# One mask product for two query thirds at the start of a block-sparse attention and spatial-gating kernel

## The chip, the cores and the metric

The kernel runs on one core of a Trainium2 chip. The metric is the device time of one execution in microseconds (us), lower is better. Three runs of the kernel before gave 209.83, 210.31 and 210.68 us; their median is 210.31 us.

The engines go by these names: PE is TensorE's matrix product and PEld its weight load, DVE is VectorE, ACT is ScalarE, POOL is GpSimd, and SP issues most of the DMA loads and stores.

## The reference

There are two stages. The first is attention over 4 batches, 8 heads, 768 positions and 64 elements a head, with a mask of blocks of 32 positions: a query block sees its own block and the two next to it, the first and the last block, and three sampled ones; the first and the last query block see all keys.

```python
scores = scale * np.matmul(q, k.transpose(0, 1, 3, 2))
mask = np.abs(blk_i - blk_j) <= window
mask = mask | (blk_i == 0) | (blk_j == 0) | (blk_i == n_blocks - 1) | (blk_j == n_blocks - 1)
for qb in range(n_blocks):
    for kb in sampled_blocks[qb]:
        mask[qb * block:(qb + 1) * block, kb * block:(kb + 1) * block] = True
scores = np.where(mask, scores, -1000000000.0)
# softmax over keys, then attn @ v
```

The second is a gated feed-forward layer on the heads put side by side (512 wide): `h = relu(x @ w_in)`, halves `u` and `v` of 512 each, `v` normalized, mixed over positions by `w_spatial` plus a bias, `(u * v_s) @ w_out`.

## The kernel before

**The mask as extra rows of the scores.** The tile `kq` holds, for each of the 8 heads of a batch, the transposed keys in columns 0 to 767 (`K_`) and the transposed queries in columns 768 to 1535 (`Q_`); partitions 0 to 63 are the head's 64 elements. Partitions 64 to 87 (`MR`; up to 127 as `MX`, zeros above 87) are 24 mask rows. Under a key they hold a one in the row of the key's block. Under a query they hold what its block adds to each key block: 0 or -300. A product of 128 rows then gives scores with the mask in them. The mask rows are the same for all heads, so they are made once, in head 0, and copied to the others by `rows` (line 236).

**How the query mask rows come about.** `bm` (24 rows, 128 columns) is the table of key blocks against query blocks, made on VectorE from the sampled blocks (line 206). `mask_rows` (line 268) multiplies it on TensorE with the one-hot key rows of a third of the positions (`TW` = 256 columns; there are three thirds) and copies the product into head 0's query columns of that third. Lines 285 to 300 write this out by hand for the first two thirds. The first product takes its one-hot rows from head 1, whose upper 64 partitions GpSimd has set to zero in columns 0 to 255 (line 173); the second takes only the 24 mask rows, from head 0. The third third follows later, in slot 3, by VectorE.

**The start.** TensorE runs 26 fillers (`filler`, line 177: products of a zero tile with itself, which nobody reads), then, in program order: transposes of head 0's keys, two fillers, the first mask product, two fillers, transposes of head 0's queries, two fillers, the second mask product, and the first scores (line 400). VectorE copies the transposes into `kq` (`split0`, line 280). ScalarE casts the first keys, copies the one-hot rows into head 0, copies the first mask product, copies head 2's key rows (columns 0 to 511; line 290), copies the second mask product, and starts on the exponentials. GpSimd casts what the loads bring in, copies the query mask rows of both thirds to head 1 (line 299) and head 2's key rows, columns 512 to 767 (line 300).

**Loads.** SP issues them in the order of the list `ORDER` (line 302), four ahead of GpSimd's casts, which go through the same list: `k1` is the keys of pair 1 (heads 2 and 3), `q1a` the first third of its queries, `v0` the values of pair 0, then `k2`, `q2a` and so on.

**Slots.** From line 840 the program goes through slots. The first 36 (`S0`) are the first batch, with 1,024 scores a partition in each: products into a `sc` bank (two of them), one exponential on ScalarE (lines 403 and 413; 424 for later batches). Lines 717 to 757 put work behind slots: `second` and `third` (the other transposes of head 0 and head 1) at slots 0 and 1, fillers at 2, the transposes `tr_first` of pairs 1, 2 and 3 at slots 4, 6 and 10, and the copies of mask rows in the list `ROWS` (line 726), all on VectorE. One entry there, `(1, 3, 4, K_)`, copies the key rows to head 3 in slot 1. Products with the values (line 451) follow four slots behind the scores, and the second stage's products (lines 554 and 623) are dealt out between them. All engines take their instructions in the order in which the program lists them.

**PSUM.** Small products and transposes share two banks, moeA and moeB; `moe_tag()` (line 253) hands them out in turn.

Of the kernel before, what the change touches and what calls it, by code (L numbers as in the profile page):

```python
# [10 lines left out]
FP32 = mybir.dt.float32  # L11
# [15 lines left out]
def kernel(  # L27
# [16 lines left out]
    nc = tc.nc  # L44

    B, H, S, D = q.shape
# [14 lines left out]
    KR = D + NB  # L61
    NT = 3
    TC = NCH // NT
    TW = TC * 128
    S0 = NT * NG * 3
    MOE0 = 12
    FILL, FILL2, FILL3 = 26, (2, 2, 2), 3
    U_DVE = (0, 1, 2, 3, 4, 5)

    const = ctx.enter_context(tc.tile_pool(name="const", bufs=1))  # L70
# [1 line left out]
    psum = ctx.enter_context(tc.tile_pool(name="psum", bufs=1, space=bass.MemoryType.PSUM))  # L72
# [10 lines left out]
    kq = const.tile([128, H, 2 * S], BF16, name="kq")  # L83
    NVV = 6
    vv = [const.tile([128, 2, NCH, VA], BF16, name=f"vv{s}") for s in range(NVV)]
    MR = slice(D, KR)
    MX = slice(D, 128)
    K_, Q_ = slice(0, S), slice(S, 2 * S)

    def qcols(t0, n=1):  # L90
        return slice(S + t0 * TW, S + (t0 + n) * TW)
# [62 lines left out]
    bm = const.tile([KR, 128], BF16)  # L154
# [15 lines left out]
    for s in range(NVV):  # L170
        nc.gpsimd.memset(vv[s][:, :, :, D:VA], 1.0)
    nc.gpsimd.memset(mhalf, -0.5)
    nc.gpsimd.memset(kq[0:D, 1, 0:TW], 0.0)

    wps = psum.tile([128, 512], FP32, tag="av", bufs=2)

    def filler(n, to):
        for _ in range(n):
            nc.tensor.matmul(out=to[:, 0:128], lhsT=warm, rhs=warm, start=True, stop=True)
# [28 lines left out]
    PL, DV = nc.gpsimd, nc.vector  # L208
# [27 lines left out]
    def rows(hs, cs, eng=nc.vector):  # L236
        src = kq[MX, 0:1, cs].to_broadcast([MX.stop - MX.start, hs.stop - hs.start, cs.stop - cs.start])
        if eng is nc.scalar:
            nc.scalar.activation(out=kq[MX, hs, cs], in_=src, func=AF.Copy)
        else:  # L240
            eng.tensor_copy(out=kq[MX, hs, cs], in_=src)
# [11 lines left out]
    def moe_tag():  # L253
        moe_tags.rotate(1)
        if moe_tags[0] in held:
            moe_tags.rotate(1)
        return moe_tags[0]

    def bank(nm="ps", tag=None):
        return psum.tile([128, 1024], BF16, tag=tag or moe_tag(), bufs=2 if tag else 1, name=nm)  # L260
# [4 lines left out]
    def pair_of(src, c):  # L265
        return src[:, c].rearrange("p h d -> p (h d)")

    def mask_rows(ps, t, copy, h=0, rs=slice(0, KR)):
        nc.tensor.matmul(out=ps[:, 0:TW], lhsT=bm[rs], rhs=kq[rs, h, t * TW:(t + 1) * TW],
                         start=True, stop=True)  # L270
        copy(kq[MX, 0, qcols(t)], ps[0:MX.stop - MX.start, 0:TW])


    def head(ps, h, c0, n, at=0):
# [5 lines left out]
    def split0(ps, h, c0, n, t, copy=dve_copy):  # L280
        w = n * 64
        copy(kq[0:D, h, c0 * 128 + t * w:c0 * 128 + (t + 1) * w], ps[t * D:(t + 1) * D, 0:w])
# [2 lines left out]
    ps0 = bank()  # L285
    head(ps0, 0, *K4)
    split0(ps0, 0, *K4, 0)
    filler(FILL2[0], wps)
    mask_rows(psum.tile([128, 1024], FP32, tag="sc", bufs=2, name="mq"), 0, act_copy, 1)
    rows(slice(2, 3), slice(0, 512), nc.scalar)  # L290
    filler(FILL2[1], wps)
    psq = bank("psq", "av")
    head(psq, 0, *Q4)
    split0(psq, 0, *Q4, 0)
    split0(ps0, 0, *K4, 1)
    filler(FILL2[2], wps)
    mask_rows(psum.tile([128, 512], FP32, tag=moe_tag(), bufs=1, name="mq"), 1, act_copy, rs=MR)
    split0(psq, 0, *Q4, 1)
    rows(H1, qcols(0, 2), PL)
    rows(slice(2, 3), slice(512, S), PL)  # L300

    ORDER = ("k1 q1a v0 k2 q2a v1 k3 q3a v2 q1b q2b r v3 q3b q0c w00 w01 w02 w03 w10 w12 w11 w13").split()
    PIECE = {"k": ALLC, "v": ALLC, "a": C01, "b": C25, "c": C45, "q": ALLC}
# [415 lines left out]
    def when(slot, *fns):  # L719
        at.setdefault(slot, []).extend(fns)  # L720

    def c(f, *a, **kw):
        return lambda: f(*a, **kw)

    K_Q0 = slice(0, S + TW)
    ROWS = [(3, 2, 8, qcols(0)), (1, 3, 4, K_), (4, 4, 6, K_), (8, 6, 8, K_),
            (15, 4, 6, qcols(1, 2)), (17, 6, 8, qcols(1, 2))]
    when(0, second)
    when(1, third)
# [1 line left out]
    for p, sl in ((1, 4), (2, 6), (3, 10)):  # L731
        when(sl, c(tr_first, p))
    for sl, h0, h1, cs in ROWS:
        when(sl, c(rows, slice(h0, h1), cs))
    for p, sl in ((2, 14), (3, 15)):
        late.setdefault(sl, []).append(c(tr_rest, p))
    when(3, lambda: mask_rows(psum.tile([128, 512], FP32, tag=moe_tag(), bufs=1, name="mq"), 2, dve_copy))
    when(16, lambda: rows(slice(1, 4), qcols(2), PL))
    for p, sl in ((1, 11), (0, 18)):
# [152 lines left out]
```

## Time and profile before

| what | time (us) |
| --- | --- |
| median of three runs | 210.31 |
| the profiled execution | 211.0 |
| its span, first to last instruction | 209.2 |
| TensorE busy in it | 203.5 (97%) |
| ScalarE busy | 168.6 (81%) |
| VectorE busy | 146.5 (70%) |
| GpSimd busy | 88.5 (42%) |
| TensorE busy from 0 to 5, 5 to 10, 10 to 13.4 | 4.03, 4.40, 3.01 |
| ScalarE busy in the same stretches | 3.02, 4.76, 2.91 |

A timeline row gives the start, the duration, the engine and line, the operation, the tile written and the tiles read, the shapes, and how many instructions it stands for; in brackets is the idle time of the engine before it and what ended it. Where a row stands for several instructions, its duration runs from the first one's start to the last one's end. Consecutive instructions of an engine overlap a little in the record. The chain of waits is followed back from the last instruction; "issue" in it is time in which nothing that the profile shows was waited for. Times in the trace count from the start of the span.

### The profile page before, as it was taken

The page shows a single profiled execution, that of the slowest core. Times are in us where ns is not written, and L with a number is a line of the kernel's source. Part 1 is how long each engine was busy: PE and PEld are TensorE (multiplying, and loading weights), DVE is VectorE, ACT ScalarE, POOL GpSimd, SP SyncE. Part 2 cuts the span into 40 slices and gives each one's busy share as a digit, 9 for nine tenths or more (in the row PEclk, how much of TensorE's full clock was granted, in tenths as well). Part 3 has the DMA queues.
Part 4 walks back from the last instruction along what each step waited for, and adds up shares of the span by engine and source line. Part 5 has one row for each costly group of instructions (what it writes and reads, how often), then busy time and mean ns, then how long its engine had stood idle before and what let it go on. Part 6 is the DMA issues. An engine that isn't in the chain of part 4 may idle for free.

```text
span 209.2 us, 5514 instructions
## 1 busy us (share of the span) xinstructions
PE 203.5 (97%) x2228; PEld 138.9 (66%) x2228; DVE 146.5 (70%) x316; ACT 168.6 (81%) x222; POOL 88.5 (42%) x184
## 2 busy tenths in 40 slices
PE   8899999999999999999999999999999999999992
PEld 7679889777766776667666577667666567445551
DVE  6788876988866766575976686456785666576871
ACT  6999999999999999989889878889899884266021
POOL 7589889867936965006657600006211000013000
PEclk9999999999999999999999999999999999999998
DMA  5999799999999999499996920499501010610016
GB/s 155 307 364 364 254 358 265 211 272 354 283 247 318 254 282 219 149 230 340 204 286 181 162 41 0 153 190 320 98 0 41 0 35 6 248 58 0 0 71 230
DMA packets 53037, 39.48 MB, mean 189 GB/s; under 512 B 33940, under 2 KB 47636, under 8 KB 53012
## 3 DMA queue, kind: packets, MB, share of 16 engines
q1 hardware_dynamic: 52580, 38.74, 70.0%
q10 hardware_dynamic: 432, 0.39, 0.6%
q8 instruction: 17, 0.28, 0.5%
q14 instruction: 8, 0.07, 0.1%
HBM read 24.77 MB, written 6.29 MB: 148 GB/s over the span
## 4 chain that ended last, share of the span: by engine, by line
PE 91%; DMA 3%; SPq 1%; ACT 1%; POOL 1%; issue 0%; ACTq 0%
PE ps L421 22%; PE ps_moe L623 19%; PE ps_moe L554 15%; PE ps_av L469 13%; PE ps L408 6%; PE ps_t L554 4%; PE ps_t L623 4%; PE ps_av L451 4%; DMA st_k<-in_k_dram 3%; PE ps_sc L623 2%; SPq L109 1%; PE ps_sc L554 1%; ACT a_all L413 1%; PE ps L263 1%; POOL nat L137 1%; PE ps_av L263 1%
## 5 line engine op out<-in xcount | busy, mean ns | idle before, releaser
L424 ACT ACTIVATE a_all<-ps 128x768 bf16<-128x768 f32 x144 | 113.2, 811 | 13.9 <-PE ps L421 6.2
L421 PE MATMUL ps<-kq 128*128 128x512 bf16 (+1 forms) x288 | 70.3, 325 | 0.0
L469 PEld LDWEIGHTS <-a_all 128*128 128x128 bf16 x864 | 46.6, 98 | 18.9
L469 PE MATMUL ps_av<-vv,a_all 128*128 128x65 bf16 x864 | 51.1, 194 | 0.0
L421 PEld LDWEIGHTS <-kq 128*128 128x128 bf16 x288 | 27.9, 97 | 23.6
L137 POOL CAST nat<-st_k 128x256 bf16<-128x256 f32 (+3 forms) x37 | 17.9, 514 | 39.7 <-DMA st_k<-in_k_dram 39.6
L413 ACT ACTIVATE a_all<-ps 128x1024 bf16<-128x1024 f32 x35 | 33.8, 1024 | 0.9 <-PE ps L408 0.5
L623 PE MATMUL ps_moe<-w_spt,vn 128*128 128x512 bf16 (+1 forms) x144 | 33.1, 325 | 0.0
L591 POOL TENSOR_SCALAR std<-mv 128x3 f32<-128x3 f32 (+1 forms) x9 | 3.4, 382 | 47.7 <-DVE mv L588 47.5
L623 PE MATMUL ps_moe<-xt,w_in_t 128*128 128x256 bf16 (+1 forms) x112 | 22.9, 302 | 0.0
L654 DVE TENSOR_TENSOR sb<-ps_moe,b_row 128x512 f32<-128x512 f32 x18 | 12.4, 690 | 14.5 <-PE ps_moe L623 14.3
L554 PE MATMUL ps_moe<-w_in_t,xt 128*128 128x512 bf16 x72 | 22.3, 378 | 0.0
L408 PE MATMUL ps<-kq 128*128 128x256 bf16 (+1 forms) x136 | 21.0, 276 | 0.7 <-DVE kq L211 0.6
L554 PE MATMUL ps_moe<-w_out_t,un 128*128 128x512 bf16 x72 | 21.1, 378 | 0.0
L137 POOL CAST vv<-st_v 128x256 bf16<-128x256 f32 (+1 forms) x36 | 18.5, 545 | 4.8 <-DMA st_v<-in_v_dram 3.8
L137 POOL CAST nat<-st_q 128x256 bf16<-128x256 f32 (+2 forms) x41 | 18.8, 488 | 1.9 <-DMA st_q<-in_q_dram 1.8
L434 DVE TENSOR_TENSOR xn<-ps_av,rc 128x384 bf16<-128x384 f32 (+1 forms) x36 | 18.5, 513 | 1.2
L623 PEld LDWEIGHTS <-vn 128*128 128x128 bf16 x192 | 15.5, 97 | 4.4
L657 DVE TENSOR_TENSOR un<-sb,un 128x512 bf16<-128x512 f32 x24 | 17.2, 718 | 1.5
L587 DVE BATCH_NORM_STATS2 stats<-vn 128x6 f32<-128x512 bf16 x24 | 16.5, 688 | 1.5 <-ACT vn L582 0.9
L211 DVE COPY osb<-ps_moe 128x512 f32<-128x512 f32 x12 | 8.3, 689 | 11.2 <-PE ps_moe L554 9.3
L185 DVE TENSOR_SCALAR vn<-ps_moe 128x512 bf16<-128x512 f32 x18 | 12.4, 688 | 4.5 <-PE ps_moe L554 4.4
(94 smaller groups left out, 245.9 us busy)
## 6 DMA issues: line engine op xcount, KB each, us to landing
st_v<-in_v_dram SPq DMA_DIRECT2D x16, 384.0 KB, 6.1
out_dram<-osb SPq DMA_DIRECT2D x23, 256.0 KB, 2.1
st_k<-in_k_dram SPq DMA_DIRECT2D x15, 384.0 KB, 4.3
st_q<-in_q_dram SPq DMA_DIRECT2D x12, 384.0 KB, 4.3
ws_f<-in_moe_w_spatial_dram SPq DMA_DIRECT2D x6, 384.0 KB, 5.3
w_f<-in_moe_w_in_dram SPq DMA_DIRECT2D x8, 256.0 KB, 5.6
w_f<-in_moe_w_out_dram SPq DMA_DIRECT2D x4, 256.0 KB, 5.7
st_q<-in_q_dram SPq DMA_DIRECT2D x3, 256.0 KB, 6.9
```

Source lines behind the costliest of these rows:

```text
L137: eng.tensor_copy(out=dst, in_=src)
L185: nc.vector.tensor_scalar(out=out, in0=in0, scalar1=s1, scalar2=s2, op0=o0, **kw)
L408: nc.tensor.matmul(out=ps[:, at:at + n * TW], lhsT=kq[:, h, ci * 128:(ci + 1) * 128], rhs=kq[:, h, qcols(t0, n)], start=True, stop=True)
L413: nc.scalar.activation(out=out, in_=ps, func=AF.Exp, scale=0.125)
L421: nc.tensor.matmul(out=ps[:, n0:n1], lhsT=kq[:, j % H, ci * 128:(ci + 1) * 128], rhs=kq[:, j % H, S + n0:S + n1], start=True, stop=True)
L424: nc.scalar.activation(out=a_ref["h", j][:, ci, :], in_=ps[:, 0:S], func=AF.Exp, scale=0.125)
L434: nc.vector.tensor_tensor(out=out, in0=ps[:, :, 0:D], in1=rc[:, 0:n].to_broadcast([128, n, D]), op=ALU.mult)
L469: nc.tensor.matmul(out=av_ref[j][:, qc, :], lhsT=a_ref["h", j][:, ci, qc * 128:(qc + 1) * 128], rhs=vv[p % NVV][:, h, ci, :], start=(ci == ...
L554: nc.tensor.matmul(out=ref["ps"][:, 0:w], lhsT=lhs(i), rhs=rhs(i), start=(i == 0), stop=(i == n - 1))
L587: nc.vector.bn_stats(out=stats, in_=self.vn[:, tcc, :])
L623: nc.tensor.matmul(out=o.rearrange("p (c t) -> p c t", c=n), lhsT=lhs(i)[:, (d0 + x) * 128:(d0 + x + 1) * 128], rhs=rhs(i), start=(i == 0) ...
L657: nc.vector.tensor_tensor(out=self.in_place(*area), in0=sb, in1=self.in_place(*area), op=ALU.mult)
```

## The change

The first two thirds of the query mask come from one product of 512 columns and one ScalarE copy of 512 columns, placed right behind the transposes of head 0's keys; it takes its one-hot rows from head 1, of which GpSimd now sets columns 0 to 511 to zero. The second product and its copy go. The six fillers in three pairs become four in one piece, behind the transposes of head 0's queries. Head 2's key rows are no longer copied by ScalarE and GpSimd at the start, but together with head 3's by VectorE in slot 1.

```diff
-    FILL, FILL2, FILL3 = 26, (2, 2, 2), 3
+    FILL, FILL2, FILL3 = 26, 4, 3
...
-    nc.gpsimd.memset(kq[0:D, 1, 0:TW], 0.0)
+    nc.gpsimd.memset(kq[0:D, 1, 0:2 * TW], 0.0)
...
-    def mask_rows(ps, t, copy, h=0, rs=slice(0, KR)):
-        nc.tensor.matmul(out=ps[:, 0:TW], lhsT=bm[rs], rhs=kq[rs, h, t * TW:(t + 1) * TW],
+    def mask_rows(ps, t, copy, h=0, n=1):
+        nc.tensor.matmul(out=ps[:, 0:n * TW], lhsT=bm, rhs=kq[0:KR, h, t * TW:(t + n) * TW],
                          start=True, stop=True)
-        copy(kq[MX, 0, qcols(t)], ps[0:MX.stop - MX.start, 0:TW])
+        copy(kq[MX, 0, qcols(t, n)], ps[0:MX.stop - MX.start, 0:n * TW])
...
     split0(ps0, 0, *K4, 0)
-    filler(FILL2[0], wps)
-    mask_rows(psum.tile([128, 1024], FP32, tag="sc", bufs=2, name="mq"), 0, act_copy, 1)
-    rows(slice(2, 3), slice(0, 512), nc.scalar)
-    filler(FILL2[1], wps)
+    mask_rows(psum.tile([128, 1024], FP32, tag="sc", bufs=2, name="mq"), 0, act_copy, 1, 2)
     psq = bank("psq", "av")
     head(psq, 0, *Q4)
     split0(psq, 0, *Q4, 0)
     split0(ps0, 0, *K4, 1)
-    filler(FILL2[2], wps)
-    mask_rows(psum.tile([128, 512], FP32, tag=moe_tag(), bufs=1, name="mq"), 1, act_copy, rs=MR)
+    filler(FILL2, wps)
     split0(psq, 0, *Q4, 1)
     rows(H1, qcols(0, 2), PL)
-    rows(slice(2, 3), slice(512, S), PL)
...
-    ROWS = [(3, 2, 8, qcols(0)), (1, 3, 4, K_), (4, 4, 6, K_), (8, 6, 8, K_),
+    ROWS = [(3, 2, 8, qcols(0)), (1, 2, 4, K_), (4, 4, 6, K_), (8, 6, 8, K_),
```

## The prediction

> **What bounds the kernel now.** I read the page first (engine shares, chain by engine), then the chain in order of time for the first 24 us, then the timeline of the same stretch engine by engine, because every edited line runs before 10 us. The chain's shares by engine, and its pieces where it leaves the start:
>
> ```profile
> PE 91%; DMA 3%; SPq 1%; ACT 1%; POOL 1%; issue 0%; ACTq 0%
> ...
> 3.57 0.47 SPq L109
> 4.04 0.04 issue
> 4.08 6.98 DMA st_k<-in_k_dram
> 11.06 0.05 issue
> 11.11 1.51 POOL nat L137 x2
> 12.62 0.05 issue
> 12.66 0.28 PE ps L263 x2
> 12.95 0.45 PE ps L408 x4
> ```
>
> TensorE sets the end from 12.66 us on. Before that the chain holds no TensorE, ScalarE or VectorE work at all: it is the row of load issues on SP, the load of pair 2's keys (issued 4.08, landed 11.06), GpSimd's two casts of pair 2, and the transposes that wait for them (`tr_first(2)`). None of these reads a tile that the change writes. The timeline of the same stretch, the edited pieces and the places where the start meets the chain:
>
> ```profile
> 4.15 0.42 PE L269 MATMUL mq<-kq,bm 88*128 88x256 bf16 x1
> ...
> 4.61 0.38 ACT L214 ACTIVATE kq<-mq 64x256 bf16<-64x256 f32 x1 [0.31 <-PE mq L269]
> ...
> 4.89 0.61 ACT L239 ACTIVATE kq<-kq 64x512 bf16<-64x512 bf16 x1
> ...
> 5.46 0.56 PEld L400 LDWEIGHTS <-kq 128*128 128x128 bf16 x4 [0.22 <-DVE kq L211]
> ...
> 6.11 0.60 ACT L403 ACTIVATE a_all<-ps 128x512 bf16<-128x512 f32 x1 [0.16 <-PE ps L400]
> ...
> 8.38 0.61 PE L408 MATMUL ps<-kq 128*128 128x256 bf16 x4 [0.60 <-DVE kq L211]
> ...
> 8.54 0.40 POOL L137 CAST nat<-st_q 128x256 bf16<-128x256 f32 x1
> ...
> 8.68 0.94 DVE L241 COPY kq<-kq 64x768 bf16<-64x768 bf16 x2
> ...
> 10.92 0.67 PE L451 MATMUL ps_av<-vv,a_all 128*128 128x65 bf16 x16 [0.23 <-POOL vv L137]
> ...
> 11.60 0.75 DVE L241 COPY kq<-kq 64x1536 bf16<-64x1536 bf16 x1
> ...
> 11.88 0.73 POOL L137 CAST nat<-st_q 128x256 bf16<-128x256 f32 x1
> 12.07 1.02 ACT L413 ACTIVATE a_all<-ps 128x1024 bf16<-128x1024 f32 x1 [0.18 <-PE ps L408]
> ...
> 12.66 0.28 PE L263 MATMUL ps<-ident,nat 128*128 128x128 bf16 x2 [0.16 <-POOL nat L137]
> ...
> 13.42 17.55 ACT L413 ACTIVATE a_all<-ps 128x1024 bf16<-128x1024 f32 x18 [0.33 <-PE ps L408]
> ```
>
> The start joins the chain late. At 10.92 TensorE waits for GpSimd's cast of the first values (a load again), at 12.66 for the cast of pair 2's queries. The exponentials on ScalarE, fed since 6.11, run dry twice: 0.18 us at 12.07 and 0.33 us at 13.42. So the start may come up to 0.18 + 0.33 = 0.51 us later before the exponential at 13.42 notices, and coming earlier only lengthens those two idles.
>
> **The change, part by part.**
>
> *Mask product, its place and width.* The two fillers ahead of it go (two starts 0.107 apart: 26 fillers took 2.96 us, less 0.31 for the last, over 25). It then waits for `bm`, which VectorE finished at 3.91 (3.74 + 0.17). VectorE to TensorE took 0.05 in the first filler (`tiny` ended 0.92, filler at 0.97), and the weight load some 0.1 more: start about 4.07 against 4.15. At this pitch 128 columns took 0.31 and 256 took 0.42, so 512 take 0.42 + 2 x 0.107 = 0.63: end 4.70 (before 4.57). Its wider zero rows are GpSimd's memset: 64x256 took 0.33 from 3.04, twice that ends by 3.71, ahead of the product and of GpSimd's next cast (3.99, waiting for a load). Hidden.
>
> *One copy on ScalarE for two.* The 64x256 copy took 0.38; the nearest rows for 512 columns are the 128x512 exponential out of PSUM (0.60) and the 64x512 copy (0.61). I take 0.60, bounds 0.38 and 0.61: it starts at 4.74 and ends at 5.34 (5.12 to 5.35), where the two copies ended at 4.99 and 5.95.
>
> *Query transposes and the first scores.* The mask's 512 columns hold TensorE for 0.43, to 4.50 (the query cast is there at 4.39). The two transposes run at 4.50 and 4.61 instead of 4.58 and 4.68, VectorE's first query copy ends at 5.23 instead of 5.31. Before, the first score product started 0.15 after that copy. Now it needs this copy (5.23 + 0.15 = 5.38) and the mask copy (5.34 + 0.05 to 0.15 = 5.39 to 5.49). So L400 at 5.38 to 5.49 against 5.46: between -0.08 and +0.03. I take -0.03, and the same for the first exponential, whose second half is no longer behind a mask copy. The second mask product (0.21 of TensorE at 5.14) is gone; the four fillers stand at 4.72 to 5.15, and the wait after them covers them. If they were not covered they would cost at most 4 x 0.107 less the 0.21 saved = 0.21.
>
> *Head 2's key rows.* 0.61 leaves ScalarE and 0.40 leaves GpSimd (64x256 at 6.80). Both had room: GpSimd next waits for pair 1's keys until 7.77, ScalarE had finished its rows before the first scores. VectorE takes them: 64x768 becomes 64x1536 at 8.68. The pair of copies took 0.94 and 64x1536 alone about 0.55 (0.56 at 15.10), so the first needed some 0.40; the new one needs 0.2 more (0 to 0.35; the high end is 0.75, the same shape at 11.60). Behind it on VectorE stand the rows at 9.08, the third mask copy (9.66), pair 1's transposed copies (10.16) and the rows at 11.60. Some 0.06 of the 0.2 is taken up by the wait for the transposes ahead of 10.16, so 10.16 becomes about 10.30. The consumer of the first copy is TensorE at 11.44, 0.6 after that copy's end (10.84); that of the second at 12.79, 1.2 after its end (11.57). Neither sees +0.15, nor +0.35. Cover gone, it would cost its 0.2.
>
> *PSUM tags.* One `moe_tag()` less swaps moeA and moeB from `ps_f` on. `ps_f` no longer waits for the bank of the key transposes; `third`'s bank then waits for the key copy that ended at 5.64 rather than the mask copy that ended at 5.95, and is wanted at 6.74. No DMA is added, dropped or moved on SP's queue. Zero.
>
> *Sum.* Start -0.03 (-0.08 to +0.03), VectorE's +0.15 hidden, all of it in front of 12.66, where the chain comes from loads: 0.0 us. The profiled execution took 211.0 (span 209.2 and 1.8 around it); the median of the three runs is 210.31, which is 0.7 less, so 211.0 - 0.7 + 0.0 = 210.3.
>
> **Two rules against the rows.** VectorE's row copy at 11.60 took 0.75 where the same shape took 0.56, and GpSimd's cast at 11.88 took 0.73 where the same shape took 0.40 at 8.54: they held each other up by 0.2 and 0.33. The Trainium skill, "SBUF — State Buffer", section Who interferes with whom, says that a 2-port VectorE copy and GpSimd exclude each other for a whole instruction, whoever issues first; these two rows agree. By that rule the sum would change only if the order flipped, which is the first rival.
>
> The granted-clock row stands at 9 from the start, yet 128-column products start every 0.107 us until 6.08 and every 0.056 after 6.25 (eight in 0.61 at 9.51). The Trainium skill, "TensorE: Matmul & The Clock Gate", section Part 1: The HAM clock gate, says that TensorE runs at half rate until it has been busy for a window of about 3.4 us that is not tied to the kernel's start. The trace agrees in the step of pitch, not in the granted clock. By that rule fewer products before 6.2 could leave one more window at half rate; that is the second rival.
>
> **The rivals.**
>
> *GpSimd goes first (faster).* If VectorE's rows of 11.60 are asked for only after GpSimd has begun its cast of 11.88, that cast takes 0.40 instead of 0.73, the transposes of 12.66 come 0.33 earlier, and the exponential of 13.42 too: 210.0. For it: my shift puts the request at 11.75. Against: VectorE must lose its place to a cast that starts at 11.88, 0.13 later still.
>
> *Half rate lasts longer (slower).* If it lasts to 9.6, where pair 1's transposes stand: from 6.25 to there TensorE has 5504 columns, 2.3 us at the fast pitch and 4.6 at the slow one. It idles 0.7 (7.66 to 8.38) and 0.4 (10.5 to 10.92), and the exponentials have 0.51: 2.3 - 0.7 - 0.4 - 0.51 = 0.7 late at 13.42 at most, and 0 at the least, because the exponentials, 0.9 each, cover half-rate scores of 0.85. I take 0.4: 210.7. It decides (over 0.5%) once half rate lasts into the full stretch after 13.4, where every us of it costs 0.5: to about 14.2 on top of the 0.7, 211.4. For it: TensorE's idle ahead of the first score products is 0.25 to 0.3 in one piece instead of two of 0.1. Against: in total that idle hardly grows, and the stretch after 6.2 is dense whatever the rate.
>
> *VectorE's queue turns up (slower).* The 0.2 becomes 0.35 and the GpSimd lock falls worse: another 0.33 on GpSimd's chain at 11.9, 210.6. Against: the copies' consumers have 0.6 and 1.2 in hand.
>
> *The change does what it says and is worth its time.* Were the loads early enough in undisturbed runs for the start to set the end, it would bring -0.08 to +0.03: 210.2 to 210.3, no other verdict.
>
> **How the numbers follow.** Nothing reaches 12.66, or the start's own -0.08 to +0.03: 0.70 (210.3). GpSimd first: 0.12 (210.0). Half rate: 0.08 (210.7), a quarter of it beyond 211.4. VectorE's queue: 0.06 (210.6). Something not seen here, of either sign: 0.04. A measurement of this kernel can tell about 0.5% (1.05 us) from no change; the three runs shown differ by 0.85. The cases run from 210.0 to 210.7, and the runs lie 0.48 below and 0.37 above their median: 209.6 to 211.0. Within 0.5% are the first, nearly all of the second and fourth and most of the third: 0.88. Slower takes the quarter of the half-rate case and most of the unseen: 0.07; faster the rest: 0.05.
>
> **What would show it.** One mask product 128x512 near 4.07 and one ScalarE copy near 0.60 ending by 5.35; L400 at 5.38 to 5.49; a 64x1536 VectorE copy near 8.7 and the transposed copies near 10.30; the chain still from SP, the key load and GpSimd into L263 near 12.66; exponentials dry at 12.07 and 13.42 as before. Wrong if a VectorE or ScalarE wait stands in that chain, if pitches of 0.107 go on after 6.5, or if the cast at 11.88 takes 0.40 or over 0.8.

## The result and the profile after

The changed kernel is slower: 211.19 us at the median of 22 runs against 210.50 for 22 runs of before, a ratio of 1.0031 (95% interval 1.0019 to 1.0042). Two later timings of the same two kernels gave 1.0015 (1.0002 to 1.0028) and 1.0010 (0.9990 to 1.0029). Over all runs the mean is 211.01 (46 runs, standard error 0.05) against 210.55 (159 runs of before, 0.04): 0.46 us. The forecast was 210.3, 209.6 to 211.0, and no change.

The two profiled executions hide this: 211.01 here, 211.0 before, with a span of 209.2 in both. That of before was an unlucky one, in the slowest eighth of its runs (20 of the 159 took 211.0 or more). The profile of the changed kernel, the chain of waits over the first 24 us, some of its longest pieces:

```profile
8.61 1.76 DVE kq L241 x2
10.40 0.42 DVE kq L211
10.85 0.69 DVE kq L211
11.59 0.62 PE ps L403 x4
12.24 2.86 ACT a_all L408 x3
```

Where before had SP, the load of pair 2's keys and GpSimd, VectorE now leads into the scores of slot 6. The timeline of the same stretch, the rows that answer to those of before (from line 300 on its lines stand five lower: L403 is before's L408, L446 its L451):

```profile
4.12 0.61 PE L269 MATMUL mq<-kq,bm 88*128 88x512 bf16 x1
...
4.77 0.59 ACT L214 ACTIVATE kq<-mq 64x512 bf16<-64x512 f32 x1 [0.47 <-PE mq L269]
...
5.38 0.56 PEld L395 LDWEIGHTS <-kq 128*128 128x128 bf16 x4 [0.28 <-ACT kq L214]
...
6.04 0.60 ACT L398 ACTIVATE a_all<-ps 128x512 bf16<-128x512 f32 x1 [0.68 <-PE ps L395]
...
8.61 1.76 DVE L241 COPY kq<-kq 64x1536 bf16<-64x1536 bf16 x2
...
9.01 0.95 POOL L137 CAST vv<-st_v 128x768 bf16<-128x768 f32 x1 [0.16 <-DMA st_v<-in_v_dram]
...
10.46 0.67 PE L446 MATMUL ps_av<-vv,a_all 128*128 128x65 bf16 x16
...
10.85 1.41 DVE L211 COPY kq<-ps 64x1024 bf16<-64x1024 bf16 x2
11.01 0.40 POOL L137 CAST nat<-st_q 128x256 bf16<-128x256 f32 x1
...
11.59 0.61 PE L403 MATMUL ps<-kq 128*128 128x256 bf16 x4 [0.46 <-DVE kq L211]
...
12.24 1.94 ACT L408 ACTIVATE a_all<-ps 128x1024 bf16<-128x1024 f32 x2 [0.43 <-PE ps L403]
```

The edited pieces fall where they were expected. But pair 0's values landed a microsecond earlier than in the profile of before (cast at 9.01, not 10.04), so TensorE is through the first products with them by 11.13 and then waits 0.46 for VectorE. VectorE's two row copies took 1.76 instead of 0.94, the second of them alone 1.18, because GpSimd's cast of those values began at 9.01 between them: the two engines held each other up, here called the lock.

A second loss is far from the edit. With the loads early, the changed kernel's execution ran 0.26 us ahead of before's from slot 8 to 46 us, and there it lost its lead within one instruction. ScalarE's timeline, the changed kernel:

```profile
44.93 1.52 ACT L419 ACTIVATE a_all<-ps 128x768 bf16<-128x768 f32 x2
46.68 1.51 ACT L419 ACTIVATE a_all<-ps 128x768 bf16<-128x768 f32 x2 [0.23 <-ACT a_all L419]
```

and before, the same exponentials without a gap:

```profile
45.90 2.24 ACT L424 ACTIVATE a_all<-ps 128x768 bf16<-128x768 f32 x3
```

The page names ScalarE itself as the releaser. In the trace, ScalarE passes a wait instruction at 46.30 and starts the exponential behind it 0.375 later; every other such pair of this stretch has 0.06. It is the pair that stands at numbers 62 and 63 of ScalarE's instructions, counted from 0.

### The profile page after: what moved, and what is told of

It is laid out like the page before. It is cut to its first block, busy times and chain, and to the rows that moved or that the text cites. A ratio compares the mean times of both kernels' runs of the same rounds, so it can differ in the third digit from the quotient of the medians.

```text
span 209.2 us, 5506 instructions
## 1 busy us (share of the span) xinstructions
PE 203.3 (97%) x2225; PEld 138.6 (66%) x2225; DVE 148.1 (71%) x316; ACT 167.9 (80%) x220; POOL 88.0 (42%) x183
## 4 chain that ended last, share of the span: by engine, by line
PE 90%; ACT 3%; DVE 2%; DMA 2%; issue 1%; POOL 1%; SPq 0%; ACTq 0%; POOLq 0%
PE ps L416 22%; PE ps_moe L618 18%; PE ps_moe L549 15%; PE ps_av L464 13%; PE ps L403 6%; PE ps_t L549 4%; PE ps_t L618 4%; PE ps_av L446 4%; PE ps_sc L618 2%; DMA st_k<-in_k_dram 2%; ACT a_all L419 1%; ACT a_all L408 1%; DVE kq L211 1%; PE ps_sc L549 1%; DVE kq L241 1%
## 5 line engine op out<-in xcount | busy, mean ns | idle before, releaser
L408 ACT ACTIVATE a_all<-ps 128x1024 bf16<-128x1024 f32 x35 | 33.7, 1024 | 0.8 <-PE ps L403 0.4
L403 PE MATMUL ps<-kq 128*128 128x256 bf16 (+1 forms) x136 | 21.0, 276 | 1.1 <-DVE kq L211 1.1
```

The lines of the kernel that those rows point to most:

```text
L403: nc.tensor.matmul(out=ps[:, at:at + n * TW], lhsT=kq[:, h, ci * 128:(ci + 1) * 128], rhs=kq[:, h, qcols(t0, n)], start=True, stop=True)
L408: nc.scalar.activation(out=out, in_=ps, func=AF.Exp, scale=0.125)
```

## The experiments

Three theories. **V**: VectorE's longer row copy, with the lock between it and GpSimd, delays pair 1's transposed copies, and only the late load in before's profiled execution had hidden that. **M**: the mask product, its copy or the fillers. **I**: the stall on ScalarE at 46 us comes with the change, because it has two ScalarE instructions fewer.

For all of them, this is what the exponentials show in each profiled execution (numbered from 0; slot 0 has two, 0 and 1, so that slot 6 has number 7): the start of number 0; the excess of the steps 6 to 7, 7 to 8 and 12 to 13 over the shortest seen; the step 42 to 43; and the time from 40 to 180.

```
kernel (run)                    ex 0   6>7   7>8  12>13  42>43  40 to 180
before                          6.11  0.31  0.45  0.00   0.729   129.53
before again (e3)               5.49  0.00  0.00  0.00   0.729   129.53
before, third mask late (e10)   6.05  0.38  0.43  0.04   0.728   129.53
changed                         6.04  0.56  0.02  0.04   1.041   129.80
changed again (e4)              5.62  0.19  0.02  0.00   1.043   129.80
changed, third time (e11)       5.88  0.00  0.00  0.13   1.043   129.80
rows only (e1)                  5.71  0.00  0.03  1.04   0.725   129.53
rows only again (e14)           5.79  0.41  0.02  0.00   0.725   129.53
rows twice (e13)                6.00  0.43  0.02  0.22   0.726   129.53
mask only (e2)                  6.04  0.00  0.00  0.00   0.726   129.53
mask only again (e15)           5.88  0.00  0.00  0.03   0.726   129.53
rows on GpSimd (e7)             6.05  0.00  0.00  0.57   1.043   129.80
one copy more (e5)              5.72  0.61  0.02  0.18   0.726   129.53
one copy more again (e12)       5.99  0.00  0.61  0.11   0.726   129.53
seven copies more (e6)          6.75  0.00  0.00  0.55   0.728   129.54
one copy, short rows (e8)       5.68  0.18  0.02  0.33   0.726   129.53
one copy, third mask late (e9)  6.09  0.00  0.00  0.68   0.726   129.53
```

The last column says that from exponential 40 on there are two times and nothing else: 129.53, and 129.80 with the step of 1.04. Everything before 40 varies with the execution, in kernels of either kind. The large values at 7 to 8 are casts of pair 2 that waited for loads. At 12 to 13 it was a load of pair 1's queries in e1; in e6, e7 and e9 TensorE waited 0.34 to 0.43 for VectorE, whose row copy near 15 had taken 0.97 to 0.99 beside a cast of GpSimd, against 0.56 free.

**e1 and e14, the rows alone** (on the kernel before; of the list `ROWS` the entry that changes is shown):

```diff
-    rows(slice(2, 3), slice(0, 512), nc.scalar)
...
-    rows(slice(2, 3), slice(512, S), PL)
...
-(1, 3, 4, K_)
+(1, 2, 4, K_)
```

> Only head 2's key rows move: VectorE copies them with head 3's (64x1536 in slot 1); mask products, mask copies and fillers stay as before. Theory V (VectorE's queue ahead of pair 1's transposed copies is what the change lengthens, and before's profiled execution hid it because its values of pair 0 landed late, near 10.0): ratio 1.003, 1.002 to 1.005; the exponential that stood at 12.07 comes near 12.2 with the scores before it waiting for VectorE. Theory M (one wide mask product, its late copy, fewer fillers cost the time): 1.000, within 0.001. Theory I (the instruction count on ScalarE shifts a stall of 0.3 us to 46.6): about half, 1.001 to 1.002.

> Head 2's key rows on VectorE and nothing else, a second time: theory V 1.0008 (1.000 to 1.0016), between before and the doubled copy and nearer to before, because its 0.2 is partly within what the sixth unit has in hand.

Both measured 1.0012 (e1 0.9998 to 1.0027, e14 0.9997 to 1.0027), medians 210.71 and 210.74. Theory V had put e1 at 1.002 to 1.005, so V alone is too little for the whole loss. ScalarE has one instruction fewer and no stall. So the rows alone cost some 0.2 us: a mean of 210.76 (24 runs, standard error 0.06). The profiled executions show it in part. In e14, TensorE waited 0.32 for GpSimd's cast of pair 0's values, which took 1.16 instead of 0.83 beside VectorE's row copies and came behind a cast of 0.73 instead of 0.40; the transposed copy for the same scores ended at 11.11, 0.09 ahead of them. Together they make its 0.41 at step 6 to 7. In e1 that step was free, the forecast wait for VectorE did not show, and the execution lost 1.04 at step 12 to 13, where GpSimd sat idle 1.26 us for a load of pair 1's queries.

**e2 and e15, the mask product, its copy and the fillers alone** (on the changed kernel):

```diff
+    rows(slice(2, 3), slice(0, 512), nc.scalar)
...
+    rows(slice(2, 3), slice(512, S), PL)
...
-(1, 2, 4, K_)
+(1, 3, 4, K_)
```

> Only the mask product, its copy and the fillers change; head 2's key rows stay on ScalarE and GpSimd. Theory V: 1.000, 0.999 to 1.001; first exponential near 6.04 as in the changed kernel, rows on VectorE 64x768 and 64x1536 as before. Theory M: 1.003. Theory I: 1.001 to 1.002.

> The mask product, its copy and the fillers alone, a second time: 1.000 (0.9992 to 1.0008). Above 1.001 would put a part of the start's loss on the mask product or the fillers.

Measured 1.0004 (0.9985 to 1.0022) and 0.9998 (0.9982 to 1.0014). Theory M falls: this half of the change is free, to within some 0.2 us (mean 210.48, 24 runs, standard error 0.10).

**e3 and e4, before and after once more**, unchanged.

> The kernel before against itself: 1.000 within 0.001 gives the noise. Its profile is a second look at when the values of pair 0 land: theory V expects an execution near the median (210.5) to have them earlier than 10.0 and the exponential after the sixth unit earlier than 12.07; if it lands near 10.0 again, theory V has no cover to point to.

> The changed kernel once more: 1.003 (1.002 to 1.0045). Its profile is a second look: theory V expects scores of slot 6 to wait for VectorE near 11.6 again and the exponential near 12.24; theory I expects the 0.3 us stall at 46.6 on ScalarE again.

e3: 1.0004 (0.9992 to 1.0017), profiled execution 209.86. The values of pair 0 were cast at 8.83, and ScalarE ran six exponentials through without a gap:

```profile
7.37 5.75 ACT L413 ACTIVATE a_all<-ps 128x1024 bf16<-128x1024 f32 x6
...
8.08 1.13 DVE L241 COPY kq<-kq 64x768 bf16<-64x768 bf16 x2
...
8.83 1.07 POOL L137 CAST vv<-st_v 128x768 bf16<-128x768 f32 x1
...
9.96 0.67 PE L451 MATMUL ps_av<-vv,a_all 128*128 128x65 bf16 x16
...
10.47 0.60 PE L408 MATMUL ps<-kq 128*128 128x256 bf16 x4
```

The chain of waits of this execution holds no load on its way to the full stretch; the first exponentials lead into it:

```profile
5.49 1.08 ACT a_all L403 x2
6.58 1.83 ACT a_all L413 x2
8.43 5.61 ACT a_all L413 x6
```

So the 0.51 us of idle on which the prediction built belongs to an execution with late loads, not to the kernel. e4: 1.0015 (1.0002 to 1.0028), the stall at the same exponential, and step 6 to 7 late by 0.19. At those scores TensorE has no wait for VectorE here. Behind the load of pair 1's keys the chain goes through GpSimd's casts, of which that of `q1a` took 0.73 instead of 0.40 and that of pair 0's values 1.15 instead of 0.83, both beside VectorE's row copies:

```profile
7.75 1.50 POOL nat L137 x2
9.25 1.11 POOL vv L137
...
10.40 0.67 PE ps_av L446 x16
11.08 0.45 PE ps L403 x4
...
11.55 2.87 ACT a_all L408 x3
```

**e5 and e12, one more ScalarE instruction** (on the changed kernel), a one-element copy where ScalarE is idle; it is called the one-copy kernel from here on:

```diff
     mask_rows(psum.tile([128, 1024], FP32, tag="sc", bufs=2, name="mq"), 0, act_copy, 1, 2)
+    act_copy(tiny, tiny)
```

> The changed kernel with one more ScalarE instruction, a copy of one element a partition onto itself, behind the mask copy where ScalarE idles 0.7 us. Theory I (a stall of 0.31 us on ScalarE between the wait and the exponential that fall on instruction numbers 62 and 63 of its trace): the pair becomes 63 and 64, the gap there is 0.06 as everywhere, and 0.3 us of the loss goes: ratio 1.0005 to 1.0015. Theory V alone (VectorE's queue at the start): nothing changes, 1.0025. The exponential after the sixth unit still waits for VectorE in either.

> The one-copy kernel a second time: 1.001 (1.000 to 1.002), 0.0012 below the changed kernel beside it (0.26 us, what the stall took between the exponentials 40 and 180). The start alone, theory V, is what is left over 1.000.

Measured 1.0004 (0.9985 to 1.0022) and 1.0008 (0.9988 to 1.0028). The stall is gone; ScalarE's row of e5 holds five exponentials without a gap:

```profile
45.13 3.68 ACT L420 ACTIVATE a_all<-ps 128x768 bf16<-128x768 f32 x5
```

Beside e12 on one chip, the changed kernel (e11) stood at 1.0010, only 0.0002 above where 0.0012 was expected. That difference alone is within the noise; the means over all runs, 211.01 (46) and 210.72 (24 runs, standard error 0.07), differ by 0.29, and the traces by 0.27. Against only the runs of before that were timed beside them, the changed kernel is 0.43 us slower (standard error 0.07), the one-copy kernel 0.10 (0.09) and the rows-only kernel 0.27 (0.08).

What is left of the loss in e5 is at the start, theory V's place; in e12 step 6 to 7 was free:

```profile
8.20 1.81 DVE L241 COPY kq<-kq 64x1536 bf16<-64x1536 bf16 x2
...
8.74 0.87 POOL L137 CAST vv<-st_v 128x768 bf16<-128x768 f32 x1 [0.24 <-DMA st_v<-in_v_dram]
...
11.24 0.61 PE L404 MATMUL ps<-kq 128*128 128x256 bf16 x4 [0.51 <-DVE kq L211]
...
11.89 1.02 ACT L409 ACTIVATE a_all<-ps 128x1024 bf16<-128x1024 f32 x1 [0.48 <-PE ps L404]
```

**e6, seven of them** (on the changed kernel).

```diff
+    for _ in range(7):
+        act_copy(tiny, tiny)
```

> Seven such copies instead of one. Theory I: the stall comes back one pair earlier, between the wait and the exponential that stood at numbers 55 and 56 in the changed kernel (near 41.5), 0.37 instead of 0.06, and not near 46. If it is gone everywhere, or stays at the same exponential, the position is not what makes it. The copies may push the first exponential by up to 0.7 us, so the time says nothing.

One run, 211.87, with the first exponential 0.7 later, as foreseen. The stall is back, one pair earlier, at another exponential and between other shapes, again behind ScalarE's instruction 62 (0.370 between the wait and the exponential); at 46 to 48 there is none:

```profile
41.56 1.02 ACT L410 ACTIVATE a_all<-ps 128x1024 bf16<-128x1024 f32 x1
42.94 1.51 ACT L421 ACTIVATE a_all<-ps 128x768 bf16<-128x768 f32 x2 [0.35 <-ACT a_all L410]
```

**e7, the rows on GpSimd** (on the changed kernel), which keeps its count of ScalarE instructions and gives VectorE its old queue:

```diff
+    rows(slice(2, 3), K_, PL)
...
-(1, 2, 4, K_)
+(1, 3, 4, K_)
```

> The changed kernel, but head 2's key rows copied by GpSimd in one piece (64x768) instead of by VectorE: ScalarE has the changed kernel's instruction count, VectorE the queue of before. Theory I: the stall of 0.31 at the same exponential (46) and ratio about 1.0013. Theory V alone: 1.000. GpSimd's longer copy ends by 8.0 and could delay its cast of pair 1's keys by 0.3, which both theories take as hidden.

Measured 1.0014 (0.9995 to 1.0033), median 210.96, with the stall where the changed kernel has it:

```profile
46.87 1.51 ACT L420 ACTIVATE a_all<-ps 128x768 bf16<-128x768 f32 x2 [0.23 <-ACT a_all L420]
```

Its mean is 0.25 us (standard error 0.13) above that of the runs of before beside it, about what the stall takes (0.27): with VectorE's old queue nothing beyond the noise is left for the start.

e6 and e7 settle theory I as to the place: it is the position in ScalarE's instructions, with or without the rest of the change.

**e8, shorter rows** (on the one-copy kernel):

```diff
-(3, 2, 8, qcols(0))
+(3, 2, 4, qcols(0))
...
+(5, 4, 8, qcols(0)),
```

> As the one-copy kernel, and VectorE's first rows of query mask cover heads 2 and 3 only (64x512); heads 4 to 7 follow in slot 5. Theories V and I together: neither stall nor late transposed copies, ratio 1.000 (0.999 to 1.0008), scores of slot 6 no longer waiting for VectorE. Theory I alone: the same as the one-copy kernel. Theory V alone: 1.001 to 1.0015.

A miss: 1.0031 (1.0010 to 1.0053). The scores of slot 6 still came 0.18 late, as the shortened copy took 0.92 beside the cast of pair 0's values. The copy that was split off stands ahead of pair 2's transposed copies and pushed those from about 12.6 (e5) to 13.63, which cost 0.45 at step 9 to 10. VectorE's queue is tight there as well; the run does not tell the theories apart.

**e9 and e10, the third mask product later** (on the one-copy kernel and on before):

```diff
-    when(3, lambda: mask_rows(
+    when(9, lambda: mask_rows(
```

> The changed kernel with the one-element ScalarE copy (no stall at 46), and the third mask product and VectorE's copy of it (0.42) moved from slot 3 to slot 9, behind pair 1's and pair 2's transposed copies. Theory V: those copies come 0.4 earlier, more than the 0.2 that the change added, so the exponential after the sixth unit follows at its free pitch of 0.90 unless the GpSimd lock costs over 0.2; ratio 0.999 to 1.0005, below the one-copy kernel by 0.0005 or more. If the start cost nothing, it equals the one-copy kernel.

> The kernel before with that third mask product moved alike. Theory V: before's VectorE queue was mostly hidden (free pitch in the second look at it), so 1.000 (0.999 to 1.0005). Clearly under 0.999 would say that VectorE's queue ahead of pair 1 set the start of before as well.

e9 1.0009 (0.9983 to 1.0036), against 1.0008 of the one-copy kernel beside it: not the gain that theory V expected, and what was named for a start that costs nothing, but with an interval that leaves room for either. Step 6 to 7 came free; its runs spread from 209.89 to 212.01. e10 0.9995 (0.9971 to 1.0018), with the values late once more (9.99). Neither settles anything.

**e11, the changed kernel a third time.**

> The changed kernel a third time, beside the next one on the same chip: 1.0025 (1.0015 to 1.0035); stall of 0.31 at the same place.

1.0010 (0.9990 to 1.0029), below the expected range; the stall as before, step 6 to 7 free.

**e13, the suspected copy twice** (on the rows-only kernel):

```diff
-(1, 2, 4, K_),
+(1, 2, 4, K_), (1, 2, 4, K_),
```

> The kernel with only head 2's key rows moved, and VectorE's 64x1536 copy in slot 1 issued twice: VectorE's queue ahead of pair 1's transposed copies is 0.55 longer than there and 0.75 longer than before. Theory V: the exponential after the sixth unit is late by 0.5 to 0.8 and the ratio 1.0025 to 1.0035. If loads cover the start, as the prediction had it: 1.000 to 1.001.

1.0031 (1.0014 to 1.0048), median 211.25, without the stall. VectorE's three row copies end at 10.04, pair 1's transposed copies start at 10.53, and GpSimd's cast of the values stretches to 1.26 where 0.83 is its free time. The chain runs through all three row copies and the copies behind them. Step 6 to 7 was 0.43 late, less than the 0.5 to 0.8 expected, and not by VectorE alone: the values' load was late too (1.09 idle ahead of the cast).

```profile
8.42 1.62 DVE L241 COPY kq<-kq 64x1536 bf16<-64x1536 bf16 x3
10.07 0.42 DVE L211 CAST kq<-mq 64x256 bf16<-64x256 f32 x1
10.53 1.41 DVE L211 COPY kq<-ps 64x1024 bf16<-64x1024 bf16 x2
```

```profile
9.48 1.26 POOL L137 CAST vv<-st_v 128x768 bf16<-128x768 f32 x1 [1.09 <-DMA st_v<-in_v_dram]
```

By VectorE's extra work in slot 1 the means are: none, 210.55 (159 runs of before); 0.2 us more, 210.74 (48 runs of the rows-only and one-copy kernels, standard error 0.05); 0.75 us more, 211.16 (9 runs, 0.14). The time follows the copy at nearly its full length.

The chains of the profiled executions agree. VectorE's row copies of slots 1 and 3, near 9 us, stand in the chain of five of the eleven with the longer copy (changed, e5, e8, e9, e13); in two more (e4, e14) GpSimd's casts stand there, stretched beside those copies; in none of the six with the old one. Theory V holds as to its cause, VectorE's longer row copy. Its path is twofold: TensorE waits for the transposed copies, or for a cast that the row copies hold up. In the other four (e1, e6, e11, e12) step 6 to 7 was free, so the 0.2 us is a mean over executions, not a delay of each.

## Why the prediction was wrong

- **Right: the mask product, the copy and the start.** Product at 4.12 (4.07 forecast) for 0.61 (0.63), copy 0.59 (0.60) to 5.36, weights of the first scores at 5.38 (5.38 to 5.49), first exponential at 6.04 (6.08). GpSimd's wider memset took 0.55 and hid. The half was worth nothing either way: 1.0004 and 0.9998.
- **Wrong, the step on head 2's key rows: "Neither sees +0.15, nor +0.35."** The 0.2 us for the longer copy was about the right size: from its start to the next one's it took 0.48 to 0.54 in e1, e11 and e12, against 0.40 in before, and up to 0.94 (e9) with the lock. The consumer's 0.6 us in hand was read off one execution, in which TensorE reached slot 6's scores at 11.44 only because pair 0's values had landed late. In e3 it reached them at 10.47, and VectorE's copy for them ended at 10.38. In hand is about 0.1. In e1, e11 and e12 the longer copy alone still fitted; with the lock it did not, and step 6 to 7 lost 0.56 (changed), 0.61 (e5) and 0.19 (e4). The mean over all runs is 0.19 us. The prediction's own "Cover gone, it would cost its 0.2" had the price, and the rival "VectorE's queue turns up" the mechanism; it got 0.06, and its margins were that same execution's.
- **The lock** worked between other instructions than the prediction watched: VectorE's second row copy against the cast of pair 0's values (1.18 against 0.55 us free in the changed kernel's profile), not the copy at 11.60 against the cast at 11.88. The Trainium skill, "SBUF — State Buffer", section Who interferes with whom, gives the whole instruction to whoever issues first; that fits 1.18 in the main: the cast still had 0.77 to go when the copy's turn came at 9.19, and with the copy's own 0.55 behind it that makes 1.32, 0.14 too much.
- **Wrong, the sum: "all of it in front of 12.66".** The larger part of the loss, 0.27 to 0.29 us, is the ScalarE stall at 46 us. Nothing in the prediction looked at what two ScalarE instructions fewer do to the ones behind; "0.61 leaves ScalarE" was taken for idle time alone, and the effect on the rest of the kernel was put at nothing without a reason. Nor does the chain come "from loads" in the kernel as such: e3 has none there.
- **Half rate and GpSimd first** did not decide anything: TensorE's pitch changed over at about 6.1 in the changed kernel's profile, as in before's, and the cast of pair 2's queries took its free 0.40 (at 11.01) without a gain. That cast at 0.40, and VectorE in the chain, are two of the signs that the prediction had named for being wrong. **The PSUM tags** cost nothing: mask only swaps them too.
- **The range** (209.6 to 211.0) came from that one profiled execution and three runs. 0.19 and 0.27 add up to the 0.46 us that all runs show. The first timing, 0.69 at the median, is the high one of three; the medians of the other two, 210.76 and 210.93, lie inside the range. So it is chance that the first lay outside it, but not that the kernel is slower.

Three things stay open. How much of the 0.19 us comes by TensorE's wait for VectorE and how much by GpSimd's casts was not measured. What is special about ScalarE's instruction 62 was not shown. The Trainium skill, "Runtime: NRT & Kernel Launch", section Instruction fetch mechanics, says that an engine's instructions are fetched in blocks and that crossing into the next is mostly hidden; a cost that shows only where a short wait instruction, not a long exponential, stands ahead of the place would fit, as a guess, but no run here shows where blocks begin. And no version beat before: mask only, the best, has a mean of 210.48 (24 runs, standard error 0.10) against 210.55, which is no difference.

## What to carry to other kernels

Read an instruction's slack from more than one execution: where a load holds the consumer, the slack is the load's, and it goes when the load lands earlier. A copy moved onto an engine that feeds the next stage in order can cost what it takes there, plus what it and GpSimd's work hold each other up: here a row copy of 0.55 us took up to 1.18, a cast of 0.83 up to 1.26. When instructions are added or removed on a busy engine, look through the whole trace for a gap that the engine is said to have caused itself; one harmless instruction more or less tells whether it hangs on position.

## What the hardware showed that was not expected

- ScalarE loses 0.31 us between instructions 62 and 63 of its trace when 62 is a wait and 63 the exponential behind it: in the changed kernel (three profiles), e6 and e7. In the others the wait of this stretch stands at 63 or 64, and the gap behind it is 0.06.
- The change of TensorE's pitch, from 0.107 to 0.056 us for a 128-column product, does not come at a set place of the kernel: at about 6.1 us in before's first profile, at 3.8 in e3, the same kernel, and at 7.0 in e9. In e3 the first exponential came at 5.49 instead of 6.11, though the query cast was 0.21 earlier there as well. In the row below, of e3, two 128-column products start 0.056 apart before 4 us:

```profile
3.89 0.28 PE L179 MATMUL wps<-warm 128*128 128x128 bf16 x2
```

- Pair 0's values, always issued by 3.6 us, were cast at any time from 8.74 (e5) to 10.04 (before).
